# Issuing sixteen stores of projected values from ScalarE in place of SyncE

## The chip, the core and the metric

The kernel runs on one core of a Trainium2 chip. The metric is the time of one execution on the device in microseconds (us). A core has five engines that run their own lists of instructions in order: TensorE (PE in the profile, with its weight loads as PEld), VectorE (DVE), ScalarE (ACT), GpSimd (POOL) and SyncE (SP). In this kernel SP does nothing but issue DMAs. An instruction waits at the head of its engine's list until its semaphores are up, and all behind it waits too.

## The reference

Two attention blocks over 2048 tokens of 512 values, with 32 heads of 16, each with its own input and weights. Block A looks back over a window of 256 tokens, block B over all of them. The outputs stand side by side.

```python
qkv = (x @ wqkv) split into q, k, v of 32 heads
scores = einsum("bhqd,bhkd->bhqk", q, k) * 16 ** -0.5
block A alone: scores = where((0 <= q - k) & (q - k < 256), scores, -1e9)
p = softmax(scores); o = einsum("bhqk,bhkd->bhqd", p, v)
out = o (heads joined) @ wo
```

## The kernel before, in words

The tokens are cut into four chunks of 512 and sixteen tiles of 128, the heads into eight groups of four. A product of float32 precision is made of three matmuls of split operands: `split` puts the rounded value and the rest into one tile (ACT writes the first half, DVE or POOL the second).

The first stage projects. `project_qk` makes a 128x512 tile of queries or keys; `end_qk` copies it from PSUM with ACT (line 301 for the first heads, 305 for later ones), takes the rest with DVE (312) or POOL (316, 317) into a tile `st`, and SP stores both into the DRAM tensor `parts` (324). Two `st` tiles are used in turn, so a copy into one waits until that tile's last store has landed. `project_v` makes a 128x512 tile of values for one token tile; `end_v` copies it from PSUM with ACT into one of two tiles `vst` (417), and a DMA stores it, 272 KB, into the DRAM tensor `vd` (426). Each block has sixteen such tiles; those of block A, the first block, are called v1 to v16 here, in the order of their copies.

From DRAM the operands come back in the layout that attention needs: queries into `oq` (398), keys into `opk` (382), values into `vt` (434). For a unit (a head group and a chunk) PE first multiplies queries and keys to find the row maxima (518, reduced by DVE in 523, 527, 528), the maxima are transposed (595), copied by ACT into `ntr` (597) and sent by DMA into spare rows of `oq` (602). PE then makes the scores (628), ACT takes the exponential into `p` (635), POOL cuts the window (645), and PE multiplies `p` with `vt` (674). The rest of a unit is the copy `ou` (685) and its store `od` (692). Block B does the same over all keys (471, 475, 628, 659).

The order of PE's work is written by hand (`ORDER_P`, `ORDER_A`), and the loads are set among it by a small model of the engines in the kernel. PE is kept full by running the projections of block A's later heads between the attention of its first heads (`half_rows`, 352, two projections at once on halves of the rows; 222 on all rows). PSUM has seven banks for all of this, so PE also waits where ACT or DVE has not yet emptied a bank.

Every DMA raises one of eight completion counters, called DMAHW0 to DMAHW7. The counters go round in the order in which the DMAs of the whole program were placed, and they are shared by all engines that issue DMAs. Before a DMA is issued, its engine waits until the DMA that used the same counter last, eight places earlier, has landed.

The functions that the diff touches, and what calls them:

Of the kernel before, what the change touches and what calls it, by code (L numbers as in the profile page):

```python
# [151 lines left out]
def attention_kernel(ctx: ExitStack, tc: tile.TileContext, xT, wqk, wv, wo, out):  # L152

    nc = tc.nc
# [11 lines left out]
    xs, ws, parts, vd, opq, mt, pts, pvt, od, rl, osp = {}, {}, {}, {}, {}, {}, {}, {}, {}, {}, {}  # L166
# [166 lines left out]
    def mark(op, t):  # L333

        since.append((t + M.load, len(since), op))
        return t
# [70 lines left out]
    def project_v(b, c, a):  # L407
        bank, ps = room()
        yield from products(ps, pairs_v(b, c, a))
        end_v(b, c, a, bank, ps)  # L410

    def end_v(b, c, a, bank, ps):

        kt = 4 * c + a
        v = vst[0]
        vst.reverse()
        op = nc.scalar.activation(v[:, :, 0:DH], ps.rearrange("p (h d) -> p h d", d=DH), AF.Copy)
        t = mark(op, M.run("ACT", 480, M.t["PE"] + WAKE, landed["v"].pop(0)))
        release(bank, t)
        ready["vd", b, kt] = M.dma(272, t)  # L420
        slots_v.pop(0)
        slots_v.append(ready["vd", b, kt])
        landed["v"].append(slots_v[-1])
        if b not in vd:
            vd[b] = dram.tile([NG // 2, S, VP], F32, name=f"vd_{b}")
        nc.sync.dma_start(vd[b][:, kt * 128:kt * 128 + 128].rearrange("p t n -> t p n"),
                          v.rearrange("p (g h) d -> p g (h d)", g=NG // 2))

    def load_v(b, p, k0, k1):
# [402 lines left out]
    def bank(n=0):  # L832
        return M.bank("u", n)
# [9 lines left out]
    def release(b, t):  # L843
        if b is not None:
            M.release(b, t)
# [26 lines left out]
    def operands(it, n=0):  # L872

        f, b, *a = it
        if f == project_qk:
            keys = [("w", b, a[0], a[1])] + [("x", b, a[2], i) for i in range(4)]
            t = (slots_st + [M.NEVER] * 2)[n] - 2700 + LAND_V
        elif f == project_v:
            keys = [("w", b, "v", i) for i in range(4)] + [("x", b, a[0], i) for i in range(4)]
            t = (slots_v + [M.NEVER] * 2)[n] - 2700 + LAND_V  # L880
        else:
            keys = [("w", b, "o", i) for i in range(4)] + [("o", b, i, a[0]) for i in range(4 if len(a[1]) == 1 else 3)]
            t = 0
        return max(t, *(ready.get(k, M.NEVER) for k in keys))
# [139 lines left out]
    while todo_a or gen[0]:  # L1024
# [13 lines left out]
        t = NEVER  # L1038
        if gen[0]:
            t = pe  # L1040
        elif x == "p":
            t = max(bank(), operands(its_a[nb]))
        elif x == "g" and stage == 0:
            t = max(bank(1), operands(its_a[nb]), operands(its_a[nb + 1], int(its_a[nb][0] == its_a[nb + 1][0])))
        elif x == "g":
            t = min(since)[0] if CHUNK * stage == 12 else pe
        elif x == "t" and nts:
            t = max(ready["nm", *nts[0]] + LOAD, bank())
        elif x == "w" and k < i:
            un, (m, pieces), a, z = flat[k]  # L1050
            t = max(*(ready.get(("v", 0, un[1] // 2, y[0]), NEVER) for y in pieces), ready["p", *un, m] + 100,
                    M.bank("o") if a else 0)
        elif x == "s" and i < k + AHEAD and (max_rows, *flat[i][0]) in made:
            t = max(bank(1), ready["q", *flat[i][0]] + LAND)
        elif x == "e":
            t = max(ready.get(("qe",), NEVER), ready.get(("ke", early[ne][2]), NEVER)) + LAND + 500
            t = max(t, M.pair(), M.t["DVE"] - 300)
        elif x == "m" and not (mxs[nm][2] and (nts or mxs[nm][0][0] and ne < len(early))):
            un, it, z = mxs[nm]
            t = max(*(ready.get(("k", *un[:2], c), NEVER) for c in (range(NQC) if un[0] else range(un[2] + 1))),  # L1060
                    ready.get(("qd", *un), NEVER)) + LAND
            t = max(t, M.pair())
# [34 lines left out]
        elif x == "e":  # L1097
            max_item(1, 0, 0, *early[ne])
            ne += 1
        elif x == "m":  # L1100
            un, it, z = mxs[nm]
            max_item(*un, *it)
            nm += 1
            if z:
                max_finish(*un)
                nts.append(un)
        elif x == "g":
            if stage == 0:
                two = its_a[nb:nb + 2]
                nb += 2  # L1110
                banks = [M.take("u") for _ in range(2)]
            half_rows(stage, [(pairs_qk if f == project_qk else pairs_v)(*a) for f, *a in two], banks)
            stage += 1
            if CHUNK * stage == 12:
                since.clear()
            elif CHUNK * stage == 24:
                stage = 0
                for (f, *a), bank_ in zip(two, banks):
                    (end_qk if f == project_qk else end_v)(*a, bank_, view(bank_))
                    made.add((f, *a))  # L1120
        else:
            if not gen[0]:
                begin(its_a[nb])
                nb += 1
            advance()
# [42 lines left out]
    while nq < 4 * len(steps):  # L1168
# [3 lines left out]
        for x in ORDER if nm < len(mx) else LAST:  # L1172
            k = ns // HG
            if x == "s" and k < len(steps):
                if ns % HG == 0:
                    t = k * STEP
# [37 lines left out]
            elif x.isdigit():  # L1214
                if 0 <= nq < 4 * len(steps):
                    g, c, kt = steps[nq // 4]
# [8 lines left out]
                if int(x) == 4 and nm < len(mx):  # L1225

                    t = k * STEP
# [37 lines left out]
```

## Time and profile before

| | us |
|---|---|
| median of three runs | 1802.63 (1800.61 to 1805.34) |
| the profiled execution | 1802.98 |
| its span | 1801.20 |
| PE busy | 1782.0 (99%) |
| DVE busy | 1508.7 (84%) |
| ACT busy | 1400.3 (78%) |
| POOL busy | 648.8 (36%) |
| all 16 stores of block A's values issued | between 22.2 and 105.6 |

All times inside the execution are counted from the start of the span. Rows of the timeline give start, duration, engine, line, operation, tiles and how often; the bracket at the end is the time for which the engine was idle before it and what ended it. PE's busy time is modelled from the starts of pipelined matmuls, so its gaps say more than its share. SP's rows are the issues of DMAs, not their transfers: when a DMA landed is seen from who waited for it. The granted clock of PE stands in the view by stretches as PEclk.

### The profile page before, as it was taken

What the parts mean: (1) busy time and instruction counts of PE and PEld (TensorE: products, weight loads), DVE (VectorE), ACT (ScalarE), POOL (GpSimd) and SP (SyncE); (2) the same over time, 40 slices, a digit from 0 to 9 for tenths busy, and PEclk for the clock granted to TensorE, in tenths of its full rate; (3) what the DMA queues carried; (4) which work ended last, traced back from release to release, by engine and by line L of the source; (5) the groups of instructions that cost most, each with busy time, mean ns of one, the idle gap of its engine ahead of it and who ended that gap; (6) DMA issues with size and microseconds to landing.
All of it is one profiled execution on the core that took longest, in us unless ns stands there. A gap on an engine that the chain in (4) does not pass through costs nothing. (4 is left out here: it accounts for less than half of the span.)

```text
span 1801.2 us, 39184 instructions
## 1 busy us (share of the span) xinstructions
PE 1782.0 (99%) x15054; PEld 909.0 (50%) x15054; DVE 1508.7 (84%) x2243; ACT 1400.3 (78%) x2750; POOL 648.8 (36%) x1334
## 2 busy tenths in 40 slices
PE   8999999999999999999999999999999999999998
PEld 6776567767754555444444444444444444444436
DVE  4756776776789776899999999999999999999901
ACT  4366676665569676899899999999999999999983
POOL 0368888655755431133400024220112422022320
PEclk9999999999999999999999999999999999999999
DMA  7766767545572223211200311130031121010012
GB/s 249 198 201 199 213 203 226 184 138 170 176 197 87 77 87 94 57 35 44 64 17 31 68 37 29 36 71 17 16 76 35 29 64 37 17 54 10 31 37 94
DMA packets 129354, 166.80 MB, mean 93 GB/s; under 512 B 23204, under 2 KB 59044, under 8 KB 129156
## 3 DMA queue, kind: packets, MB, share of 16 engines
q1 hardware_dynamic: 129168, 164.31, 31.2%
q8 instruction: 118, 1.93, 0.4%
q14 instruction: 68, 0.56, 0.1%
HBM read 94.49 MB, written 68.19 MB: 90 GB/s over the span
## 5 line engine op out<-in xcount | busy, mean ns | idle before, releaser
L635 ACT ACTIVATE p<-ps_all 128x512 f32<-128x512 f32 x2432 | 1260.1, 597 | 183.6 <-PE ps_all L628 117.7
L475 DVE TENSOR_REDUCE mt<-ps_all 128x2 f32<-128x1024 f32 x1516 | 1195.2, 866 | 62.7 <-PE ps_all L471 51.3
L628 PE MATMUL ps_all<-oq,opk 51*128 51x512 f32 (+2 forms) x2752 | 768.1, 404 | 4.7 <-ACT p L635 3.4
L471 PE MATMUL ps_all<-opk,oq 48*128 48x512 f32 x2016 | 674.0, 438 | 0.1
L659 PE MATMUL ps_all<-p,vt 128*17 128x256 f32 (+1 forms) x6056 | 586.2, 460 | 1.7 <-ACT ou L685 1.7
L628 PEld LDWEIGHTS ps_all<-oq,opk 51*128 51x128 f32 x2752 | 395.1, 185 | 180.2 <-ACT p L635 152.0
L471 PEld LDWEIGHTS ps_all<-opk,oq 48*128 48x128 f32 x2016 | 308.9, 184 | 314.3 <-DVE mt L475 174.8
L645 POOL TENSOR_SCALAR_AFFINE_SELECT p<-p 128x256 f32<-128x256 f32 x480 | 178.7, 408 | 166.7 <-ACT p L635 165.1
L659 PEld LDWEIGHTS ps_all<-p,vt 128*17 128x17 f32 x6056 | 101.5, 95 | 227.7 <-issue 215.3
L545 POOL TENSOR_TENSOR mu<-mt 128x16 f32<-128x16 f32 x31 | 6.8, 220 | 509.4 <-DVE mt L475 509.4
L527 DVE COPY_PREDICATED ps_all<-mone,ps_all 128x256 f32<-128x256 uint16 x224 | 95.2, 425 | 82.8 <-PE ps_all L518 80.3
L528 DVE TENSOR_REDUCE nm<-ps_all 128x2 f32<-128x512 f32 x224 | 155.2, 693 | 7.7
L713 POOL TENSOR_TENSOR rd<-ld,minus 128x32 f32<-128x32 f32 x15 | 81.9, 5458 | 216.7 <-DMA ld<-od 216.7
L352 PE MATMUL ps_all<-x,w 64*128 64x512 f32 x744 | 126.0, 392 | 0.0
L222 PE MATMUL ps_all<-x,w 128*128 128x512 f32 x396 | 101.9, 406 | 1.6 <-ACT x L170 1.0
L518 PE MATMUL ps_all<-opk,oq 48*128 48x384 f32 (+2 forms) x512 | 92.5, 362 | 4.2 <-DVE st L312 2.4
L674 PE MATMUL ps_all<-p,vt 128*17 128x384 f32 (+2 forms) x1408 | 94.7, 386 | 0.7 <-POOL p L645 0.5
L352 PEld LDWEIGHTS ps_all<-x,w 64*128 64x128 f32 x744 | 89.9, 185 | 9.5 <-issue 0.4
L222 PE MATMUL ps_all<-w_o,x_o 128*128 128x512 f32 x384 | 92.8, 396 | 1.1 <-ACT ob L778 1.1
L222 PEld LDWEIGHTS ps_all<-x,w 128*128 128x128 f32 x396 | 73.2, 191 | 24.1 <-issue 2.9
L305 ACT ACTIVATE raw<-ps_all 128x512 f32<-128x512 f32 x56 | 32.2, 596 | 68.2 <-PE ps_all L222 55.5
L222 PEld LDWEIGHTS ps_all<-w_o,x_o 128*128 128x128 f32 x384 | 70.6, 188 | 26.5 <-issue 8.4
(77 smaller groups left out, 950.8 us busy)
## 6 DMA issues: line engine op xcount, KB each, us to landing
parts<-st SPq DMA_DIRECT2D x64, 512.0 KB
oq<-parts SPq DMA_DIRECT2D x128, 128.0 KB
opk<-parts SPq DMA_DIRECT2D x128, 128.0 KB
od<-ou SPq DMA_DIRECT2D x64, 256.0 KB
vd<-vst SPq DMA_DIRECT2D x32, 272.0 KB
oq<-parts SPq DMA_DIRECT2D x128, 64.0 KB
opk<-parts SPq DMA_DIRECT2D x128, 64.0 KB
t<-od SPq DMA_DIRECT2D x32, 256.0 KB
```

The costliest lines, as they stand in the source:

```text
L222: nc.tensor.matmul(ps, l(u), r(v), start=start and k == 0, stop=stop and k == n - 1)
L352: op = nc.tensor.matmul(view(banks[a ^ turn]), l(u)[rows], r(v)[rows], start=turn == q == 0, stop=turn == 1 and q == 11)
L471: nc.tensor.matmul(ps[:, n], q[rows, 128 * qt:128 * qt + 128], k[rows, kc * QC:kc * QC + QC], start=True, stop=True)
L475: op = nc.vector.tensor_reduce(out=m[:, a:a + len(heads), r, qt, kc], in_=ps, axis=AX.X, op=ALU.max)
L518: nc.tensor.matmul(two[:, a, 0:w], opq[b, g, c][rows, r, 128 * qt:128 * qt + 128], opk2(g)[rows, r, t0:t1], start=True, stop=True)
L527: nc.vector.copy_predicated(two[:, :, 256:384], later, two[:, :, 0:128])
L528: op = nc.vector.tensor_reduce(out=m[:, :, r, qt, 0], in_=two[:, :, 128:384], axis=AX.X, op=ALU.max)
L628: nc.tensor.matmul(ps[x][:, col:col + n1], opk2(g)[rows, pr, 128 * k:128 * k + 128], opq[b, g, c][rows, pr, q0:q0 + n1], start=True, stop= ...
L635: op = nc.scalar.activation(p[:, a0 + x, :w], ps[x][:, :w], AF.Exp, scale=SCALE)
L645: nc.gpsimd.affine_select(out=v, in_=v, pattern=[[0, 2], [sign, 128]], compare_op=ALU.is_ge, fill=zero_fill, base=base, channel_multiplier ...
L659: nc.tensor.matmul(o[32 * j:32 * j + VW, q0:q1], vt[(g // 2) % 2][:, kt, vc:vc + VW], pts[1, g, c, kt, j // 2][:, j % 2, q0:q1], start=kt ...
L674: nc.tensor.matmul(o[32 * j:32 * j + VW, q0:q0 + w], vt[(g // 2) % 2][:, kt, vc:vc + VW], pts[b, g, c, m, j // 2][:, j % 2, col:col + w], ...
```

## The change

The store of a value tile of block A is issued by ScalarE's own queue, right behind the copy that fills the tile. For block B it stays with SP.

```diff
@@ def end_v(b, c, a, bank, ps): @@
-        nc.sync.dma_start(vd[b][:, kt * 128:kt * 128 + 128].rearrange("p t n -> t p n"),
+        (nc.sync if b else nc.scalar).dma_start(vd[b][:, kt * 128:kt * 128 + 128].rearrange("p t n -> t p n"),
                           v.rearrange("p (g h) d -> p g (h d)", g=NG // 2))
```

The lists of PE, DVE and POOL keep their instructions and their order. SP's list loses sixteen rows and ACT's gains them. Since DMAs now come from two engines, they are placed in another order among each other, and so the counters fall to other DMAs. Three places follow. The rows are an engine's list in order, with the semaphores that an instruction waits for in brackets: DMAHW are the counters, the others are engines.

The first place is SP's list where the first queries and keys of block A are loaded back and the last chunk of the input (`in_3`) is fetched, about 20 to 30 us. Before:

```order
L426 DMA vd_261<-vst_79 128x4x136 [waits DMAHW5_49,Activation_49]
L398 DMA oq_0_0_268<-parts_0_0_199 16x2x512 [waits DMAHW6_49,DMAHW3_49]
L398 DMA oq_0_0_268<-parts_0_0_199 32x2x512 [waits DMAHW7_49]
L398 DMA oq_0_0_268<-parts_0_0_199 16x2x512 [waits DMAHW0_49]
L398 DMA oq_0_0_268<-parts_0_0_199 32x2x512 [waits DMAHW1_49]
L324 DMA parts_0_1_234<-st_0_1_1_231 128x2x512 [waits DMAHW2_49,DVE_49]
L382 DMA opk_75<-parts_0_1_234 32x2x512 [waits DMAHW4_49]
L382 DMA opk_75<-parts_0_1_234 16x2x512
L382 DMA opk_75<-parts_0_1_234 32x2x512 [waits DMAHW5_49]
L382 DMA opk_75<-parts_0_1_234 16x2x512 [waits DMAHW6_49]
L426 DMA vd_261<-vst_80 128x4x136 [waits DMAHW7_49,Activation_49]
L185 DMA in_3_0_288<-xT_A 128x2x512 [waits DMAHW0_49]
```

And after the change:

```order
L398 DMA oq_0_0_268<-parts_0_0_199 16x2x512 [waits DMAHW5_49,DMAHW3_49]
L398 DMA oq_0_0_268<-parts_0_0_199 32x2x512 [waits DMAHW6_49]
L398 DMA oq_0_0_268<-parts_0_0_199 16x2x512 [waits DMAHW0_49]
L398 DMA oq_0_0_268<-parts_0_0_199 32x2x512 [waits DMAHW2_49]
L324 DMA parts_0_1_234<-st_0_1_1_231 128x2x512 [waits DMAHW4_49,DVE_49]
L382 DMA opk_75<-parts_0_1_234 32x2x512 [waits DMAHW5_49]
L382 DMA opk_75<-parts_0_1_234 16x2x512 [waits DMAHW6_49]
L382 DMA opk_75<-parts_0_1_234 32x2x512 [waits DMAHW0_49]
L382 DMA opk_75<-parts_0_1_234 16x2x512 [waits DMAHW1_49]
L185 DMA in_3_0_288<-xT_A 128x2x512 [waits DMAHW2_49]
L185 DMA in_3_2_290<-xT_A 128x2x512 [waits DMAHW3_49]
```

The stores of v1 and v2 are gone from between the loads. The counters that SP's rows skip (7, 1, 3) went to the stores of v1, v2 and v3 on ACT, so the last `opk` row waits for v2's store (DMAHW1) and the second `in_3` row for v3's store (DMAHW3).

The second place is about 55 to 65 us, where the third query tile (`st_0_0_2`) is stored. SP's list before:

```order
L602 DMA oq_0_0_268<-ntr_0_0_507 3x8x128 [waits DMAHW6_49]
L324 DMA parts_0_0_199<-st_0_0_2_499 128x2x512 [waits DMAHW7_49,DVE_49]
L426 DMA vd_261<-vst_80 128x4x136 [waits DMAHW0_49,Activation_49]
L324 DMA parts_0_0_199<-st_0_0_3_545 128x2x512 [waits DMAHW1_49,DVE_49]
L185 DMA in_2_1_569<-wqk_A 128x512 [waits DMAHW2_49]
L398 DMA oq_0_2_601<-parts_0_0_199 16x2x512 [waits DMAHW7_49,DMAHW3_49]
```

After the change SP has:

```order
L602 DMA oq_0_0_268<-ntr_0_0_507 3x8x128 [waits DMAHW7_49]
L324 DMA parts_0_0_199<-st_0_0_2_499 128x2x512 [waits DMAHW0_49,DVE_49]
L324 DMA parts_0_0_199<-st_0_0_3_545 128x2x512 [waits DMAHW1_49,DVE_49]
L185 DMA in_2_1_569<-wqk_A 128x512 [waits DMAHW2_49]
L398 DMA oq_0_2_601<-parts_0_0_199 16x2x512 [waits DMAHW3_49,DMAHW0_49]
```

and ACT, in the same stretch (v8 is the `vst` copy here):

```order
L301 ACTIVATE st_0_0_3_545<-ps_all 128x512 [waits DMAHW2_49,PE_49]
L417 ACTIVATE vst_80<-ps_all 128x32x16 [waits DMAHW4_49]
L426 DMA vd_261<-vst_80 128x4x136 [waits DMAHW0_49,Activation_49]
L301 ACTIVATE st_0_1_3_567<-ps_all 128x512 [waits DMAHW0_49,DVE_49,PE_49]
L635 ACTIVATE p_0_0_0_0_575<-ps_all 128x512 [waits DVE_49,PE_49]
```

The store of `st_0_0_2` stood ahead of v8's store and now has the counter (0) that v8's store raised just before it, so SP holds it until v8's store has landed. ACT's copy of `st_0_1_3` reuses that `st` tile and waits for this same counter, for the store of `st_0_0_2`.

The third place is SP's list about 85 to 92 us, ahead of the second load of `vt`. Before, from the store of v13 on:

```order
L426 DMA vd_261<-vst_79 128x4x136 [waits DMAHW7_49,Activation_49]
L382 DMA opk_76<-parts_0_1_234 32x2x512 [waits DMAHW0_49]
L382 DMA opk_76<-parts_0_1_234 16x2x512 [waits DMAHW1_49]
L382 DMA opk_76<-parts_0_1_234 32x2x512 [waits DMAHW2_49]
L382 DMA opk_76<-parts_0_1_234 16x2x512 [waits DMAHW3_49]
L434 DMA vt_77<-vd_261 128x4x136 [waits DMAHW4_49]
L602 DMA oq_0_2_601<-ntr_0_2_904 3x8x128 [waits DMAHW5_49,Activation_49]
```

After the change:

```order
L382 DMA opk_76<-parts_0_1_234 32x2x512 [waits DMAHW7_49]
L382 DMA opk_76<-parts_0_1_234 16x2x512 [waits DMAHW0_49]
L382 DMA opk_76<-parts_0_1_234 32x2x512 [waits DMAHW1_49]
L382 DMA opk_76<-parts_0_1_234 16x2x512 [waits DMAHW2_49]
L382 DMA opk_76<-parts_0_1_234 32x2x512 [waits DMAHW3_49]
L382 DMA opk_76<-parts_0_1_234 16x2x512 [waits DMAHW4_49]
L434 DMA vt_77<-vd_261 128x4x136 [waits DMAHW5_49]
```

Of these counters, 7 was last used by v13's store and 4 by v14's store on ACT. Before the change v14's store stood behind the `vt` load in SP's list; now the last `opk` row, just ahead of the `vt` load, waits until it has landed.

## The prediction

> **What bounds the kernel now.** I read the page first, then the chain that ended last, then the gaps of PE up to 110 us, since all sixteen stores lie there.
>
> ```profile
> PE 1782.0 (99%) x15054; PEld 909.0 (50%) x15054; DVE 1508.7 (84%) x2243; ACT 1400.3 (78%) x2750; POOL 648.8 (36%) x1334
> PE 1%; ACT 0%; issue 0%; ACTq 0%
> L426 SPq DMA_DIRECT2D vd<-vst x32: 359/376/1736, 22.2 to 438.4; - x32
> ```
>
> PE is the bound. The chain breaks off after 1% of the span, so it says nothing of the projections; what a microsecond there is worth must be read from PE's gaps. PE's order doesn't change, so a time by which PE waits longer or shorter is carried to the end. The third row, of the `vd` tensor, prices an issue on SP: 376 ns in the median, 1736 at most. From 15 to 110 us PE has two gaps:
>
> ```profile
> 34.96 2.88 PE L222 MATMUL ps_all<-w_v,x 128*128 128x512 f32 x12
> 40.21 0.61 PE L518 MATMUL ps_all<-opk,oq 48*128 48x128 f32 x4 [2.37 <-DVE st L312]
> 40.75 4.61 PE L222 MATMUL ps_all<-w_v,x 128*128 128x512 f32 x12
> ...
> 64.89 0.93 PE L518 MATMUL ps_all<-opk,oq 48*128 48x384 f32 x2 [0.37 <-ACT p L635]
> ```
>
> The first costs more than its 2.37 us. The same twelve matmuls take 2.88 us ahead of it and 4.61 behind it, and the stretches show why (PE's busy time first, PEclk, DMA share and GB/s last):
>
> ```profile
> 37.55:40.96 3.41, 1.04 (x7) 0.68 (x6) 2.27 (x6) 2.12 (x4) 0.00 (x0) 1.00 0.62 211
> 40.96:44.37 3.41, 3.41 (x9) 2.66 (x9) 0.93 (x8) 0.00 (x0) 0.00 (x0) 0.50 0.97 288
> ```
>
> After a stretch of 3.41 us with 1.04 busy, the clock is 0.50 for one stretch: 4.61 - 2.88 = 1.73 us more. So a stall of some 2.4 us has cost 4.1 here.
>
> **The gain at 38 us.** What PE waits for there:
>
> ```profile
> 28.23 0.38 SPq L426 DMA_DIRECT2D vd<-vst  x1
> 28.65 1.07 SPq L185 DMA_DIRECT2D in<-xT_A  x2
> 32.73 0.60 ACT L417 ACTIVATE vst<-ps_all 128x512 f32<-128x512 f32 x1 [2.41 <-DMA vd<-vst]
> 35.69 1.15 ACT L170 ACTIVATE x<-in 128x512 fp32r<-128x512 f32 x2 [2.37 <-DMA in<-xT_A]
> 37.60 1.15 ACT L170 ACTIVATE x<-in 128x512 fp32r<-128x512 f32 x2 [0.75 <-DMA in<-xT_A]
> 38.65 0.57 ACT L301 ACTIVATE st<-ps_all 128x512 fp32r<-128x512 f32 x1
> 39.47 0.68 DVE L312 TENSOR_TENSOR st<-ps_all,st 128x512 fp32r<-128x512 f32 x1
> ```
>
> ACT stands behind the two `in_3` loads, issued at 28.65 behind SP's wait for v1 and its eight loads; they take 7.0 us and more to land. Then the key copy, DVE's rest, a free bank. Without v1's store SP issues the queries some 3 us sooner, so less is queued ahead of the input. But the first `in_3` load still comes behind a row that waits for v2's store (issued on ACT at 25, landing at 28 to 29.5 by the spans below), and the second waits for v3's (copied at 27.05, so landing at 30.4 to 32.2). The first is issued about when it was, the second 1.5 to 3 us later, into an emptier queue. Such a load lands 3 to 5 us after issue if the queue isn't full (2.7 for half the size, below; 7.0 when full), so between 33.4 and 37.2: I take 36. ACT's split then ends at 37.1, and from the start of the key copy to PE's start it is 1.56 (38.65 to 40.21), so PE goes on at 38.6 to 38.7. Gain 1.6 us (ends: 0 us, if the second load is as late as now, and 2.4). A gap of under 1 us leaves its stretch over two thirds busy; so the 1.7 us of slow clock go too (end: 0). Sum: -3.3 us, ends 0 and -4.1.
>
> **The loss at 64 us.** This is the term on which the sign rests.
>
> ```profile
> 58.06 0.38 SPq L324 DMA_DIRECT2D parts<-st  x1
> ...
> 59.77 0.59 ACT L417 ACTIVATE vst<-ps_all 128x512 f32<-128x512 f32 x1
> 60.39 0.36 SPq L426 DMA_DIRECT2D vd<-vst  x1
> 61.61 0.36 SPq L324 DMA_DIRECT2D parts<-st  x1
> 62.85 1.66 PE L352 MATMUL ps_all<-w_v,x 64*128 64x512 f32 x12
> 63.75 0.60 ACT L301 ACTIVATE st<-ps_all 128x512 fp32r<-128x512 f32 x1 [3.39 <-DMA parts<-st]
> 64.24 1.08 ACT L635 ACTIVATE p<-ps_all 128x512 f32<-128x512 f32 x2
> ```
>
> ACT already waits 3.39 us here for the store issued at 58.06, and PE's 0.37 us at 64.89 come from the exponentials behind it: no slack. After the change SP issues that store only when v8's store has landed, on the same counter. v8's copy ends at 60.36, so it goes out at 60.4. How long a store takes to land is bounded by these rows (a 256 KB load at the start, a 256 KB store followed by the load that waits for it):
>
> ```profile
> 0.79 0.39 SPq L185 DMA_DIRECT2D in<-wqk_A  x1
> 3.46 0.63 ACT L170 ACTIVATE w<-in 128x512 fp32r<-128x512 f32 x1 [1.40 <-DMA in<-wqk_A]
> 354.08 0.34 SPq L692 DMA_DIRECT2D od<-ou  x1
> 356.98 0.66 SPq L706 DMA_DIRECT2D ld<-od  x1
> ```
>
> 2.7 us at the least and 2.9 for the store; a store of values issued at 28.23 into a full queue had landed by 32.73 (4.5), the 512 KB one of 58.06 by 63.75 (5.7). Since SP is held, the queue runs empty: I take 2.9 for each. 60.4 + 2.9 + 2.9 = 66.2, and with 0.1 for the two releases ACT's copy starts at 66.3, not 63.75: +2.6 us on PE (ends 2.1 and 6.9). The queries of chunk 2 come later by it too, but PE, their reader, is as late.
>
> **The loss at 96 us.**
>
> ```profile
> 87.54 2.80 SPq L382 DMA_DIRECT2D opk<-parts  x4
> 90.38 0.42 SPq L434 DMA_DIRECT2D vt<-vd  x1
> 91.59 0.60 ACT L417 ACTIVATE vst<-ps_all 128x512 f32<-128x512 f32 x1 [2.91 <-PE ps_all L222]
> 93.43 0.46 SPq L426 DMA_DIRECT2D vd<-vst  x1
> 95.66 1.71 PE L674 MATMUL ps_all<-p,vt 128*17 128x128 f32 x28
> ```
>
> The `vt` load leaves at 90.38 today and is read by the ninth matmul of the row at 95.66, at 95.9. After the change the key load ahead of it waits for v14's store: copy done at 92.19, landing 2.9 later at 95.1, one key issue of 0.42, and the load lands 2.9 after 95.6, at 98.5: +2.6 us (ends 2.1 and 5.8). SP is held in the same way for v12 and v13, but the keys that wait then are read much later, beyond 110 us.
>
> **What ACT pays.** Each store costs ACT the overlap with the next copy (two copies in 1.08 us where one takes 0.60: 0.12), the issue (0.38 as on SP) and a restart, for which I put 0.1. No row shows an issue on ACT: ends 0.1 and 1.7 us each. Most of the sixteen fall into idle time of ACT. Two places have no cover:
>
> ```profile
> 74.55 1.08 ACT L417 ACTIVATE vst<-ps_all 128x512 f32<-128x512 f32 x2 [0.58 <-ACT p L635]
> 75.52 0.27 ACT L597 ACTIVATE ntr<-ps_all 64x128 f32<-64x128 bf16 x1
> 75.77 0.19 PEld L628 LDWEIGHTS ps_all<-oq,opk 51*128 51x128 f32 x2 [0.21 <-ACT vst L417]
> 87.93 0.30 PEld L518 LDWEIGHTS ps_all<-opk,oq 48*128 48x128 f32 x4 [0.42 <-ACT ntr L597]
> ```
>
> v10 and v11 follow each other, PE's next score matmul wants their banks and the projection behind it wants `ntr`'s: 1.1 us. At 87.93 PE wants the `ntr` bank behind v13: 0.5. For v14 and v16, ahead of exponentials, I add 0.3 each. +2.2 us (ends 0.3 and 6).
>
> **Clock, and the row of ones.** Two stalls of 2.6 us can each bring a slow stretch (1.73), depending on where the stretches of 3.41 us fall; I count one: +1.7 (0 to 3.5). The Trainium skill ("TensorE: Matmul & The Clock Gate", Part 1: The HAM clock gate) has the clock fall only after a whole idle window of about 3.4 us and calls the window free-running. The trace here disagrees on the first point, since a window 31% busy was enough; by the page this term would be 0 and the sum 1807.4. The rows of ones and maxima for PE's first scores at 62 us are now sent behind a wait for v7's store; no row shows PE waiting for them today: +0.3 (0 to 1.5, half a landing).
>
> SP saves 16 x 0.38 = 6.0 us of issuing. I cost it at nothing elsewhere, for SP bounds nothing but the loads above.
>
> **Sum.** -3.3 + 2.6 + 2.6 + 2.2 + 1.7 + 0.3 = +6.1 us. The profiled execution took 1802.98 (span 1801.20 and 1.78 around it), 0.35 over the median of 1802.63. So 1809.1; I say 1809.
>
> **Rivals.**
>
> *Not slower: the gain alone.* It needs the counters not to hold SP at 64 and 96 us, that is, v8's store landing and the next one too within 3.3 us after 60.4. For it speaks that these bytes no longer queue behind SP's; against it, two landings of 2.7. With the losses gone and ACT's issues hidden: 1802.98 - 3.3 = 1799.7, at best 1798.9. That is 0.2%. Chance 0.12, of which 0.04 for a gain beyond 0.3%, through shorter waits on SP that I can't see.
>
> *Nothing.* Only SP's 6.0 us of issuing move, or gain and losses cancel: 1803. Chance 0.20. The Trainium skill ("DMA: Bandwidth & Descriptors", Issuing engines are not separate DMA queues) says that all issuers share the same 16 DMA engines and that spreading saves only the issuing time. No row here has two issuers.
>
> *Much slower.* Two queues on the same 16 engines make each store land in 4.5 and 5.7 us as in the full stretches. Then the losses are 6.9 and 5.8 and both slow stretches come: 1802.98 - 3.3 + 6.9 + 5.8 + 2.2 + 3.5 + 0.3 = 1818. For it: the DMA share of 0.97 at 41 to 44 us; against it: SP is held, so less is in flight. Chance 0.16.
>
> *The change doing something else* is excluded: the lists show all sixteen rows moved.
>
> **How the numbers follow.** The case of the sum has 0.52: its own range is 1804 to 1814, and three quarters of it lie more than 0.3% (5.4 us, about what a measurement of this kernel can tell from no change) above 1802.63. Slower: 0.39 + 0.16 = 0.55. Same: 0.13 + 0.20 + 0.08 = 0.41. Faster: 0.04. The range reaches to the gain alone and into the much slower case: 1800 to 1816.
>
> **What would show it.** In the changed profile PE's gap at 40 us is under 1 us and no stretch of 0.50 follows; ACT's key copy at about 61 to 67 us waits 5 to 6 us for the store of `parts`; PE has a gap of 2 to 3 us in the row of L674 at about 96; ACT's issues stand as rows of some 0.4 us. The prediction is wrong if ACT's issue takes a microsecond or more, if the input of chunk 3 still lands at 37.6, or if stores land sooner than 2.7 us.

## The result, and the profile after

The changed kernel takes 1812.68 us in the median of eight runs (1808.57 to 1821.63), against 1802.86 for eight runs of the kernel before: a ratio of 1.0067, with a 95% interval of 1.0055 to 1.0079, or 9.8 us. The forecast was 1809, between 1800 and 1816. The direction was right and the time lies in the range; the total is 3.7 us short, and the largest error is in one term, the gain at 38 us. The profiled execution took 1812.47 us (span 1810.7), 0.2 under the median.

Two lines of the page and of the view of line 426 answer to those shown of before:

```profile
PE 1784.4 (99%) x15054; PEld 910.0 (50%) x15054; DVE 1509.2 (83%) x2243; ACT 1400.8 (77%) x2750; POOL 651.1 (36%) x1334
L426 ACTq DMA_DIRECT2D vd<-vst x16: 366/366/433, 22.0 to 112.5; - x16
```

PE is busy 2.4 us longer and the span is 9.5 us longer, so most of the time went into waits. An issue on ACT takes 366 ns, against 376 on SP. What SP waits for has changed: in the view of its waits from 15 to 110 us, line 426 waited 16.1 us for ACT's copies before (17.4 in a second profile, described below); now its other rows wait 32.8 us for stores of values (`vd<-vst`) to land (24.1 us in the loads of keys, 6.2 in one store of `parts`, 1.3 in the input, 1.2 in the ones).

Of the changed kernel's timeline, the rows with PE's gaps and the rows of ACT and SP that explain them, in order of time:

```profile
22.03 0.38 ACTq L426 DMA_DIRECT2D vd<-vst  x1
26.75 0.60 ACT L417 ACTIVATE vst<-ps_all 128x512 f32<-128x512 f32 x1 [3.64 <-DMA vd<-vst]
27.39 0.37 ACTq L426 DMA_DIRECT2D vd<-vst  x1
28.27 2.12 SPq L185 DMA_DIRECT2D in<-xT_A  x2
35.38 1.15 ACT L170 ACTIVATE x<-in 128x512 fp32r<-128x512 f32 x2 [1.46 <-DMA in<-xT_A]
37.99 0.51 PE L518 MATMUL ps_all<-opk,oq 48*128 48x128 f32 x4 [2.06 <-DVE st L312]
...
42.05 6.00 SPq L382 DMA_DIRECT2D opk<-parts  x4
48.15 0.70 SPq L280 DMA_DIRECT2D one_d<-vt  x1
53.87 1.69 SPq L602 DMA_DIRECT2D oq<-ntr  x2
58.02 0.37 ACTq L426 DMA_DIRECT2D vd<-vst  x1
60.70 0.66 PE L628 MATMUL ps_all<-oq,opk 51*128 51x384 f32 x3 [0.71 <-issue]
61.84 0.91 SPq L324 DMA_DIRECT2D parts<-st  x2
64.74 0.60 ACT L301 ACTIVATE st<-ps_all 128x512 fp32r<-128x512 f32 x1 [6.76 <-DMA parts<-st]
65.88 0.93 PE L518 MATMUL ps_all<-opk,oq 48*128 48x384 f32 x2 [2.85 <-ACT p L635]
...
84.76 15.31 SPq L382 DMA_DIRECT2D opk<-parts  x12
96.12 0.43 ACTq L426 DMA_DIRECT2D vd<-vst  x1
100.12 0.43 SPq L434 DMA_DIRECT2D vt<-vd  x1
103.10 1.70 PE L674 MATMUL ps_all<-p,vt 128*17 128x384 f32 x24 [2.64 <-DMA vt<-vd]
```

- *64 us, as forecast.* v8's store goes out at 58.02; SP sends the store of `st_0_0_2` only at 61.84, 3.8 us later, where before it went at 58.06. ACT's copy waits 6.76 us for it, PE 2.85.
- *96 us, as forecast.* SP's keys stretch over 15.31 us, held by the stores of v12, v13 and v14. v14's goes out at 96.12, the `vt` load at 100.12, and PE waits 2.64 us.
- *60 us, not forecast at this size.* The third of the four key loads at 42.05 shares its counter with v6's store, so the row of ones leaves SP at 48.15, and PE waits 0.71 us ahead of its first scores, most likely for ones and maxima.
- *38 us, forecast wrongly.* The gap is still 2.06 us. v1's store, out at 22.03, blocks the tile that v3's copy needs until 26.75; v3's store goes at 27.39, and the second `in_3` load waits for it. Its split starts at 35.38, so the load landed within the forecast's 33.4 to 37.2. It didn't help, because PE came earlier too.

By stretches (PE's busy time first, PEclk, DMA share and GB/s last), cut at the grid of 3.41 us on which the changes of the clock seen in this profile lie:

```profile
36.20:39.61 3.41, 1.62 (x9) 1.38 (x10) 2.59 (x9) 1.30 (x3) 0.00 (x0) 1.00 0.62 215
39.61:43.02 3.41, 3.41 (x11) 2.19 (x10) 0.34 (x4) 0.06 (x1) 0.00 (x0) 0.50 0.73 215
63.50:66.91 3.41, 0.98 (x8) 0.72 (x9) 0.75 (x2) 2.09 (x4) 0.52 (x2) 1.00 1.00 309
66.91:70.33 3.42, 3.42 (x19) 2.95 (x16) 1.31 (x3) 1.61 (x3) 3.42 (x7) 0.50 1.03 321
101.04:104.46 3.42, 1.36 (x24) 0.60 (x24) 0.61 (x4) 0.26 (x1) 1.13 (x3) 1.00 0.74 250
104.46:107.87 3.41, 3.41 (x40) 2.79 (x34) 1.20 (x8) 1.67 (x4) 1.13 (x3) 1.00 0.45 157
206.86:210.27 3.41, 2.25 (x22) 1.50 (x19) 3.20 (x7) 3.07 (x7) 1.65 (x2) 1.00 0.98 279
210.27:213.69 3.42, 3.42 (x10) 2.65 (x9) 1.84 (x6) 1.24 (x3) 3.42 (x10) 0.50 0.90 261
```

The stalls at 38 and 64 us are each followed by a slow stretch, the one at 101 isn't, and one comes at 210 us, where the second profile of before has one too (at 199.35 us, by the same matmuls).

### The profile page after: what moved, and what is told of

Same layout as the page of the kernel before. It is cut to its first block, busy times and chain, and to the rows that moved or that the text cites. A ratio compares the mean times of both kernels' runs of the same rounds, so it can differ in the third digit from the quotient of the medians.

```text
span 1810.7 us, 39167 instructions
## 1 busy us (share of the span) xinstructions
PE 1784.4 (99%) x15054; PEld 910.0 (50%) x15054; DVE 1509.2 (83%) x2243; ACT 1400.8 (77%) x2750; POOL 651.1 (36%) x1334
## 5 line engine op out<-in xcount | busy, mean ns | idle before, releaser
L674 PE MATMUL ps_all<-p,vt 128*17 128x384 f32 (+2 forms) x1408 | 94.3, 386 | 2.9 <-DMA vt<-vd 2.6
```

What stands on the lines that cost most here:

```text
L674: nc.tensor.matmul(o[32 * j:32 * j + VW, q0:q0 + w], vt[(g // 2) % 2][:, kt, vc:vc + VW], pts[b, g, c, m, j // 2][:, j % 2, col:col + w], ...
```

## Experiments

The theory: a store on ACT costs what its completion counter does to SP, because the DMA eight places later, mostly one of SP's, can't go before the store has landed. The rivals: two issuers compete for the DMA engines, or an issue on ACT is dear; then each store would cost about a sixteenth of the loss. The same kernel's time also varies with the clock. Over 89 runs of the kernel before, the time lies between 1797.9 and 1810.3 us and the mean granted clock between 1.000 and 0.993; a straight line through them, 1798.5 us and 1.39 us more for each 0.001 of clock, leaves 1.1 us unexplained. So the table also gives the median with each run brought to full clock by that line; the clock in it is the median of the runs' mean clocks. Since the clock is known to 0.001, differences below some 0.7 us in that column mean nothing, and it takes off the slow stretches that a stall itself brings with the others, so it can understate what a store costs. Where an expectation speaks of time net of slow stretches, it takes off the time multiplied by (1 - clock), that is 1.8 us for each 0.001: on that scale the kernel before stands at 1796.8, the changed one at 1806.2.

| stores on ACT | edit beside that | median us | ratio to before (95%) | mean clock | at full clock |
|---|---|---|---|---|---|
| none | | 1803.0 | | 0.997 | 1798.3 |
| 16 | | 1812.7 | 1.0067 (1.0055 to 1.0079) | 0.9965 | 1807.8 |
| 16 | one load of ones later | 1814.7 | 1.0065 (1.0053 to 1.0077) | 0.994 | 1806.4 |
| 15, not v8 | | 1815.1 | 1.0064 (1.0052 to 1.0076) | 0.993 | 1805.6 |
| 15, not v14 | | 1811.1 | 1.0046 (1.0034 to 1.0058) | 0.996 | 1806.5 |
| 15, not v14 | one load of ones later | 1809.7 | 1.0036 (1.0022 to 1.0051) | 0.996 | 1803.6 |
| 14, not v8, v14 | | 1809.0 | 1.0041 (1.0029 to 1.0053) | 0.997 | 1805.0 |
| 11, nor v10, v11, v13 | | 1809.9 | 1.0026 (1.0010 to 1.0042) | 0.9945 | 1801.8 |
| 7, v1 to v7 | | 1809.3 | 1.0023 (1.0009 to 1.0038) | 0.994 | 1800.8 |
| 1, v8 | | 1807.2 | 1.0024 (1.0012 to 1.0035) | 0.9945 | 1799.6 |
| none | the kernel before again | 1801.5 | 0.9991 (0.9975 to 1.0007) | 0.9975 | 1797.8 |
| none | one load of ones later | 1802.3 | 0.9992 (0.9980 to 1.0005) | 0.9965 | 1797.9 |
| none | v1's store later | 1801.8 | 0.9992 (0.9978 to 1.0005) | 0.997 | 1797.7 |
| none | both later | 1800.3 | 0.9979 (0.9965 to 0.9993) | 0.997 | 1796.3 |

The medians are over all of a kernel's runs (5 to 12, and 89 for the first row), the ratios from runs side by side on one chip. PE's instructions and their order are the same in all these kernels. So there is a measure that leaves out what the clock does elsewhere: the time from one row of PE to another. The rows are the four of twelve matmuls in line 222 that start at 56.58, 64.92, 85.64 and 98.64 us in the second profile of before (shown below). One profile of each kernel, in us; a star marks a slow stretch inside, worth 1.5 to 1.7 us each:

| stores on ACT | 57 to 65 us | 65 to 86 us | 86 to 99 us |
|---|---|---|---|
| none, both profiles of before | 8.4, 8.3 | 20.7, 20.7 | 13.0, 13.0 |
| 16 | 13.3* | 22.1 | 16.4 |
| 16, one load of ones later | 8.1 | 23.2 | 18.0* |
| 15, not v8 | 13.3** | 22.5 | 18.1* |
| 15, not v14 | 13.6* | 22.2 | 14.4 |
| 15, not v14, one load of ones later | 8.9 | 24.0 | 13.7 |
| 14, not v8, v14 | 9.6 | 22.3 | 14.2 |
| 11, nor v10, v11, v13 | 9.9 | 20.8 | 13.1 |
| 7, v1 to v7 | 10.3 | 20.7 | 13.0 |
| 1, v8 | 12.0* | 20.7 | 13.0 |

Which stores ACT issues is chosen by one condition, here in short for the second experiment (12 is v8's token tile; the kernel lists the other fifteen). Where an edit adds lines, line numbers shift: 527 and 535 below are 518 of the kernel before, 644 and 652 are 635, 315 is 312, 326 is 324, 377 is 372, 435 is 426, 683 is 674. The condition:

```diff
-        (nc.sync if b else nc.scalar).dma_start(vd[b]...
+        (nc.scalar if b == 0 and kt != 12 else nc.sync).dma_start(vd[b]...
```

**The store at 64 us: another neighbour, all sixteen stores on ACT.** One load of ones, not needed soon, is put off, so that it takes the place eight behind v8's store:

```diff
@@ load_ones @@
+            if (g, a) == (1, 1):
+                put_off.append(ones)      # ones() is the same dma_start
+            else:
+                ones()
@@ end_qk, behind the store into parts @@
+            if (b, p, s, c) == (0, 0, 0, 2):
+                put_off.pop()()
```

> All sixteen stores stay on ScalarE. Only one of the four loads of the row of ones (opk<-one_d) is moved on SP from ahead of the store of st_0_0_2 to behind it, so that the store no longer shares its counter with v8's store. Theory (shared counter): PE's gap of 2.85 us at 63 us falls to under 0.6, ACT's copy of st_0_1_3 waits under 4.5 us instead of 6.76 for the store of parts, the slow stretch at 67 to 70 us goes, and the time falls from 1812.7 by 2.5 + 1.5 to about 1808.5. Rival (two issuers compete for the DMA engines, or ScalarE's issue is slow): nothing changes, 1812 to 1813, and the gap stays above 2 us.

Its timeline:

```profile
57.00 0.39 SPq L326 DMA_DIRECT2D parts<-st  x1
59.36 0.37 ACTq L435 DMA_DIRECT2D vd<-vst  x1
63.32 0.27 SPq L377 DMA_DIRECT2D opk<-one_d  x1
63.55 0.93 PE L527 MATMUL ps_all<-opk,oq 48*128 48x384 f32 x2 [0.18 <-ACT p L644]
```

The store of `st_0_0_2` leaves at 57.00, before v8's; now the load of ones is held, from 57 to 63.32. PE's wait there falls from 2.85 to 0.18 us. ACT's copy waits 3.08 us instead of 6.76, no slow stretch follows, and PE takes 8.1 us from 57 to 65 us, as before the change, instead of 13.3. That is the counter: both issuers, their sixteen stores and their bytes are as they were. But the time, expected at 1808.5, was 1814.74. The clock was lower in those five runs (0.994 against 0.9965); at full clock the kernel gains 1.4 us, not 2.5. Its profile has half speed for 30.7 us of its span, against 10.2 in the changed kernel's, 10.2 of them at 535 us, where nothing was edited, and 3.4 behind the wait for `vt` at 100 us, which had none in the changed kernel. A new wait of 0.60 us for queries came at 70 us.

**The same store, v8 on SP.**

> Fifteen stores on ScalarE, v8's store back on SP, behind the store of st_0_0_2 as before. Theory (shared counter at 64 us): as with the load of ones moved: gap at 64 us under 0.6 us, no slow stretch behind it, about 1808.5. Rival (contention or the cost of issues on ScalarE): one sixteenth of the loss, 0.6 us, goes: 1812.

```profile
62.89 0.88 PE L628 MATMUL ps_all<-oq,opk 51*128 51x384 f32 x3 [2.94 <-issue]
```

No gap is left at 64 us, but PE's first scores wait 2.94 us, where they waited 0.71 in the changed kernel, and two slow stretches follow where none was expected. The profile names no releaser for this wait; that it is for ones and maxima, the operands sent last, is an inference. So the expected 1808.5 was missed at 1815.12, and 2.2 us are gained at full clock. Removing one wait at this place uncovered the other.

**The keys at 96 us, v14 on SP.**

> Fifteen stores on ScalarE, v14's store back on SP, where it stands behind the second load of vt as before. Theory (shared counter at 96 us): the key load ahead of the vt load waits no longer for v14's store; PE's gap of 2.64 us at 100 us falls to under 0.5; about 1809.7. The gap at 64 us stays at 2.5 to 3 us. Rival: 1812.

```profile
104.27 1.70 PE L674 MATMUL ps_all<-p,vt 128*17 128x384 f32 x24 [1.18 <-DMA vt<-vd]
```

The gap falls from 2.64 to 1.18, not under 0.5: v12's and v13's stores still hold key loads ahead of `vt`. The gap at 64 us stays, at 2.88, as expected. 1811.07, 1.3 us less at full clock.

**Both on SP, and with v10, v11 and v13 as well.**

> v8's and v14's stores back on SP, fourteen on ScalarE. Theory: both stalls and the slow stretch go, 1812.7 - 4.0 - 2.9 = 1805.8; what is left over 1802.9 is ScalarE's issuing (about 2 us) and the late row of ones at 60 us (0.7). If the whole loss came from those two counters, 1803 or less. Rival (contention): 1811 to 1812.

> As the run with v8 and v14 back on SP, with v10, v11 and v13 back on SP too, so eleven stores on ScalarE. Theory (these three issues are not covered): the gap of 0.3 to 0.5 us at the maxima's copy (about 76 to 79 us) and 1.3 to 1.6 us in all go: 1807.5, and 1803.5 net of slow stretches less 1.4. Rival (ScalarE's issues cost nothing on PE's path): no change against 1809.0.

With v8 and v14 back the time was 1808.96, not 1805.8: 2.8 us gained at full clock. With v10, v11 and v13 back too, the median didn't move (1809.93, at a lower clock), but at full clock 3.2 us more are gained, twice the 1.4 expected for ACT's issues alone. Its profile has neither the gap at the maxima's copy nor the one of `vt`, which was still 0.92 with v13 on ACT. The rows of PE show where: 1.5 us between 65 and 86 us, where ACT's issues of these stores lie, as expected, and 1.1 between 86 and 99. So v13's share is most likely in part a hold on SP, and the wait at 96 us belongs to v13 and v14 together; v10, v11 and v13 were not moved one by one.

**Both neighbours gone.** The load of ones put off, and v14 on SP:

> Fifteen stores on ScalarE, v14's on SP, and the last load of the row of ones moved on SP behind the store of st_0_0_2, so that neither v8's nor v14's store shares a counter with what PE waits for. Theory: of the loss against the kernel before only the late input (0.6 to 1.8 us) and ScalarE's issues (2.5 us) are left, with slow stretches as often as in the run with the ones alone: PE has no gap over 1.3 us from 45 to 115 us, and the time net of slow stretches is 1800 to 1801.5, against 1803.6 with v14 on ScalarE and 1796.8 before. Rival (two issuers compete in themselves): 1803 net and more.

```profile
71.22 0.88 PE L527 MATMUL ps_all<-opk,oq 48*128 48x384 f32 x2 [1.35 <-DMA oq<-parts]
98.84 1.70 PE L683 MATMUL ps_all<-p,vt 128*17 128x384 f32 x24 [0.44 <-DMA vt<-vd]
```

1809.71, and 1801.4 net of slow stretches, as expected; 4.2 us less than with the whole change at full clock, though fifteen stores still go out from ACT. From 57 to 99 us PE takes 46.5 us, against 51.8 with the whole change and 42.1 before. A new wait of 1.35 us for queries, 0.05 over the expected limit, has come in.

**The first term alone: v1 to v7 on ACT.**

> Only the first seven stores go out from ScalarE, the other nine stay on SP. The prediction's first term alone: gain of 3.3 us, 1799.5. New theory: the gap at 38 us doesn't shrink (the second in_3 load waits for v3's store, whose copy waits for v1's store), and the rows of ones come no sooner: 0 to 1.5 us slower than before, 1802.5 to 1804, PE's gap at 36 to 40 us between 2 and 3 us.

```profile
38.91 0.51 PE L518 MATMUL ps_all<-opk,oq 48*128 48x128 f32 x4 [3.25 <-DVE st L312]
62.76 0.64 PE L628 MATMUL ps_all<-oq,opk 51*128 51x384 f32 x3 [1.85 <-issue]
```

Forecast as a gain of 3.3 us, it is a loss: ratio 1.0023, 2.5 us at full clock, more than the new theory's 1.5 at most. The gap at 38 us is 3.25 in this execution, and the first scores wait 1.85 us: the theory had the row of ones come no sooner, and it comes later (at 49.99 us against 45.79 in the second profile of before).

**One store alone.** With only v8 on ACT, the counter falls to another DMA, the second load of maxima:

> Only v8's store goes out from ScalarE, fifteen stay on SP. In this order of DMAs it shares its counter with the second load of the maxima's rows (oq<-ntr), not with the store of st_0_0_2. Theory (shared counter): SP holds that load until v8's store has landed at 60 to 62 us, it lands 2.1 to 2.5 later, and PE's first scores (L628) wait for it: a gap of 3 to 4 us at about 60 to 64 us that the kernel before hasn't; with it 3 to 6 us slower than before, 1805 to 1808. Rival (each store on ScalarE costs one sixteenth of the loss): 0.6 us slower, 1803.

```profile
58.79 7.63 SPq L602 DMA_DIRECT2D oq<-ntr  x2
62.93 0.40 ACTq L426 DMA_DIRECT2D vd<-vst  x1
67.97 0.41 PE L628 MATMUL ps_all<-oq,opk 51*128 51x384 f32 x2 [2.72 <-DMA oq<-ntr]
```

SP's two loads of maxima take 1.69 us in the changed kernel and 7.63 here: the second can't go until the store of 62.93 has landed. PE waits 2.72 us at the place named beforehand, with 3 to 4 expected, and takes 3.7 us more than before from 57 to 65 us, a slow stretch included. One store costs 0.24% (0.12 to 0.35), against 0.6 us, 0.03%, by the rivals. At full clock it is 1.3 us, less than the gap: that column also takes off the stretch behind the gap, and the profile has other slow stretches that come before the store, at 11 us and from 41 to 48 us.

**The kernel before, a second profile.**

> The kernel before once more, for a second profile of it. Its first profile had two slow stretches ahead of 45 us (10.24 and 40.96), which may hide what the loads of ones and maxima cost. Theory (PE meets those loads whenever it is early enough): in a profile without the slow stretch at 10 us, PE has a gap of 0.5 to 2 us ahead of its first scores (L628) at about 60 us, the gap at 38 us is 3 us or more, since the input lands when it did, and the time net of slow stretches differs little. If the slow stretch at 10 us is there again, the profile repeats the first within 0.5 us up to 110 us.

```profile
33.15 2.90 PE L222 MATMUL ps_all<-w_v,x 128*128 128x512 f32 x12
37.50 0.61 PE L518 MATMUL ps_all<-opk,oq 48*128 48x128 f32 x4 [1.44 <-DVE st L312]
38.04 4.59 PE L222 MATMUL ps_all<-w_v,x 128*128 128x512 f32 x12
...
45.79 0.70 SPq L280 DMA_DIRECT2D one_d<-vt  x1
56.58 2.99 PE L222 MATMUL ps_all<-x,w 128*128 128x512 f32 x12
62.03 0.93 PE L518 MATMUL ps_all<-opk,oq 48*128 48x384 f32 x2 [0.35 <-ACT p L635]
64.92 3.02 PE L222 MATMUL ps_all<-w_v,x 128*128 128x512 f32 x12
76.66 3.02 PE L222 MATMUL ps_all<-w_v,x 128*128 128x512 f32 x12
85.64 3.02 PE L222 MATMUL ps_all<-w_v,x 128*128 128x512 f32 x12
98.64 3.01 PE L222 MATMUL ps_all<-w_v,x 128*128 128x512 f32 x12
```

This execution has no slow stretch at 10 us, and PE's row ahead of the gap at 38 us starts 1.8 us earlier (33.15 against 34.96). I expected a longer gap there and a new one at 60 us. Neither came: the gap is 1.44 us, since ACT's copies, and with them the stores and the input, are earlier too. So the gap has no one size: with the first seven stores on SP, it is 2.37 us in the first profile and 3.49 in the run with v8 alone, each with a slow stretch at 10 us ahead of it, and 1.44 here and 1.01 with the load of ones later, both without one. A slow stretch follows the gap of 1.44 (4.59 for twelve matmuls), none that of 1.01 (3.04).

**What the change was credited with, done without it.** SP stood still for v1's copy while other DMAs were ready. A cure is to move v1's store on SP, not to another engine. The next runs do so, and put off the load of ones as above, each by itself and both together:

```diff
@@ end_v, all stores on nc.sync, in a function send @@
+        if (b, kt) == (0, 1):
+            put_off.append(send)
+        else:
+            send()
@@ end_qk, behind the store into parts @@
+            if (b, p, s, c) == (0, 0, 1, 1):
+                put_off.pop()()
```

> The kernel before, all stores on SP, with one edit: the last of the four loads of the row of ones is moved behind the store of st_0_0_2. If these loads hold back the maxima's rows and the store of parts in the kernel before too, PE's gaps at 60 to 65 us go and the time falls by 0.5 to 1.5 us, 1801 to 1802; if the kernel before has slack there, no change.

> All stores on SP as before; only the store of v1 is moved on SP from ahead of the four loads of queries to behind them and the store of st_0_0_1_1, so that SP doesn't stand still for v1's copy while other DMAs are ready. This is what the change was credited with at 38 us, without a second issuer. Theory: the last input chunk is issued about 3 us sooner (25 us instead of 28) and lands by 33, PE's gap of 1.4 to 2.4 us at 36 to 40 us goes, with the slow stretch behind it: 1.4 us, at most 3.1, faster than before, 1799 to 1801. Rival (the input is late because the DMA engines are full, not because SP stood still): gap as before, no change.

> No store on ScalarE. On SP the store of v1 is moved behind the loads of queries and the store of st_0_0_1_1, and the last load of the row of ones behind the store of st_0_0_2. Each alone moved the time by -0.1% at most (ratios 0.9992 and 0.9992, neither apart from 1). Theory: the first takes away most of the gap at 36 us and pushes 0.6 us of it into the wait for the maxima at 57 us, the second takes that one away: 1.5 us and a slow stretch less, 1799.5 to 1801.5 against 1803. Rival: what is won is waited for again somewhere up to 205 us, and no gain can be measured.

Neither alone can be told from no change: with the load of ones put off, nothing waits for it in the kernel before; with v1's store later (1801.8 us, 1799 to 1801 expected) the input was issued at 25.54, the gap at 38 us fell to 0.48 with no slow stretch behind it, and 0.56 of it came back as a wait of the first scores at 57 us. Both together, in the profile:

```profile
24.77 1.02 SPq L185 DMA_DIRECT2D in<-xT_A  x2
36.59 0.61 PE L535 MATMUL ps_all<-opk,oq 48*128 48x128 f32 x4 [0.78 <-DVE st L315]
60.04 0.93 PE L535 MATMUL ps_all<-opk,oq 48*128 48x384 f32 x2 [0.47 <-ACT p L652]
```

The input goes out at 24.77 instead of 27.58 in the second profile of before, the gap is 0.78, no slow stretch follows it, and the wait at 57 us is gone. 1800.31 us, ratio 0.9979 (0.9965 to 0.9993): 0.2% faster than the kernel before. Where the gain comes from is not shown: in its profile PE is 1.9 us ahead of the second profile of before at 99 us, but in the profile with the load of ones alone, which had no slow stretch either at 38 us, it is 2.0 ahead, and that kernel's time could not be told from before.

## Why the prediction was right or wrong

The second profile of before and the changed kernel's are alike up to 30 us (both without the early slow stretch), so PE's rows can be laid side by side. The changed kernel's counterparts of the rows above, the first behind the gap at 38 us, the last behind the keys:

```profile
56.97 3.03 PE L222 MATMUL ps_all<-x,w 128*128 128x512 f32 x12
70.30 2.99 PE L222 MATMUL ps_all<-w_v,x 128*128 128x512 f32 x12
83.03 3.02 PE L222 MATMUL ps_all<-w_v,x 128*128 128x512 f32 x12
92.38 3.07 PE L222 MATMUL ps_all<-w_v,x 128*128 128x512 f32 x12
108.74 3.06 PE L222 MATMUL ps_all<-w_v,x 128*128 128x512 f32 x12
```

Starts of the same row, after minus before: +0.4 (56.97 - 56.58), +3.9 (65.88 - 62.03), +5.4, +6.4, +6.7, +10.1; the spans differ by 10.3.

| step of the prediction | forecast | measured | from |
|---|---|---|---|
| gain at 38 us | -3.3 | +0.4 | lag at 57 us |
| row of ones | +0.3 | +0.7 | PE's gap at 60 us |
| loss at 64 us | +2.6 | +2.5 | gap 2.85 - 0.35 |
| clock behind it | +1.7 | +1.5 | lag 65.9 to 70.3 us |
| loss at 96 us | +2.6 | +2.6 | gap at 103 us |
| what ACT pays | +2.2 | +2.1 | lag 1.0 and 0.4 (to 92 us), 0.7 of 3.4 (to 109 us) |
| sum | +6.1 | +9.8 | |

The step that failed is the first, "Gain 1.6 us ... the 1.7 us of slow clock go too". Its landing was right (36 forecast, the split starts at 35.38), as was PE's restart (38.6 forecast, 37.99). What failed is what they were set against. I held PE's arrival at 37.84 and the input's old landing at 37.6, from an execution with a slow stretch ahead of them; in the changed kernel's PE arrives at 35.93. In an execution of before without that stretch the input is early too: ACT starts its last two splits at 34.88, and PE goes on at 37.50, half a microsecond before the changed kernel's. So that the forecast landing agreed is luck: the change made the input land later, not sooner. v2's store now stands ahead of the first input load, and v3's, whose copy had to wait for v1's store, ahead of the second. One pair of profiles doesn't give the size: without the early slow stretch PE goes on at 37.18 and 37.50 in two profiles with these stores on SP, and between 37.79 and 39.01 in five with them on ACT. The run with v1 to v7 alone shows the sign over twelve runs. The 3.7 us that the sum in this table is short lie here; some 0.3 us of the lag of 10.1 is in no row.

The two losses and ACT's issues came out within 0.1 us in the profile, the first of them in part by luck. From v8's copy to ACT's copy of `st_0_1_3` it is 7.35 us (57.39 to 64.74), against 3.90 in the second profile of before (57.00 to 60.90): SP's hold is worth 3.45 us, not 2.6, since v8's store kept SP for 3.8 us and not 2.9. PE felt 2.5 there because it was already 0.8 later by its wait at 60 us. So the two waits aren't independent: with v8's store back on SP the wait at 60 us grew to 2.94. I had asked of each stall what is late next, and not done it for this one. The row of ACT is what is left of the lag, 1.4 us of it from 65 to 86 us; that part vanished when v10, v11 and v13 went back to SP (22.3 to 20.8 us). The row of ones was mis-sized: I looked only at v7's hold, while v6's store holds SP ahead of it, in the keys, and the row of ones leaves SP at 48.15 us against 45.79.

Of the signs named, ACT's wait (6.76 us, longer than the 5 to 6 forecast), the gap of 2.64 in the row of L674 and issues of 0.37 us came; "under 1 us and no stretch of 0.50" at 40 us did not, although the input landed well before 37.6.

Of the rivals, the gain alone is refuted by its own run. "Nothing" is refuted by the time: the issuers were tied to each other by completion counters, and the run with one store on ACT costs 0.24%. The Trainium skill ("DMA: Bandwidth & Descriptors", Issuing engines are not separate DMA queues) says that a second issuer saves only issuing time; that leaves out what decided here. "Much slower" did not come: the held store was sent 3.8 us after v8's, and ACT could copy 2.9 us after that, not 4.5 and 5.7. The clock term came out of the trace: stretches with PE busy for 0.98, 1.62 and even 2.25 of 3.41 us were followed by half speed, and 1.5 us was measured behind the stall at 64 us. The Trainium skill ("TensorE: Matmul & The Clock Gate", Part 1: The HAM clock gate) has half speed in its table of states after a whole idle window. By that rule the clock term would have been 0.

## What to carry to other kernels

Before a DMA is moved to another engine, list which DMA uses its completion counter next and which engine will stand waiting for it: a transfer that nobody needed soon can become the one that holds a whole queue. Take the slack at a place from more than one execution where the clock changes between them, and credit a shorter wait only up to the next thing that is late. If a queue stands still because its next DMA isn't ready, first try to move that DMA behind ready ones on the same queue.

## What was not expected of the hardware

The granted clock varies from run to run by more than this change is worth. The kernel before ran between 1797.9 us at a mean clock of 1.000 and 1810.3 at 0.993, with the same instructions. Nor does PE's busy share of the stretch before decide: 2.25 of 3.41 us was followed by half speed, 1.36 (with one idle piece of 2.06, from 101.04 to 103.10) by full speed. What does decide stays open; no run varied it by itself. A gap of 0.5 us in line 628 stands at 525.79 in the first profile of before and is followed by full speed; at the same matmuls, the second profile of before has one slow stretch behind it (gap at 523.51), the one with the load of ones put off three (at 534.21). So of kernels that differ by less than 5 us, PE's gaps and the clock must be read beside the median.
